# Ten and six weight chunks for the first token tile, with new transfer costs in the planner

## The chip, the cores and the metric

The kernel runs on one core of one Trainium2 chip. Its time is device microseconds from the first to the last instruction of the program, and the median of three runs of the kernel before is 1571.47 us (1571.19 to 1572.18). The engines are TensorE (PE, with PEld for its weight loads), VectorE (DVE), ScalarE (ACT), GpSimd (POOL) and SyncE (SP), which here only issues transfers.

## The reference

An attention with pooled keys and values feeds two feed-forward layers, each `x @ w_in`, an activation, `@ w_out`:

```
k_p, v_p = mean of k, v over groups of 8 positions        # 576 -> 72 keys
attn = softmax(q @ k_p.T / 8) @ v_p                       # 8 batches, 8 heads, 576 x 64
x = attn as 4608 tokens x 512
x = leaky(x @ w_in1, 0.01) @ w_out1                       # 512 -> 2048 -> 512
x = h * clip(h + 3, 0, 6) / 6 @ w_out2, with h = x @ w_in2
```

The weights arrive as 64-bit words and are decoded to float32 on the chip. The kernel makes every large product of three matmuls on split operands (high x high, high x low, low x high).

## The kernel before

The 4608 tokens are nine tiles of 512. Tiles 0 to 2 go through the first layer with ordinary matmuls, one chunk of 128 hidden units after the other (`gemm1` makes a chunk's hidden values, `activate` and `split_g` turn them into `gh` and `gl`, and two steps later `gemm2` adds the chunk's share to four output banks `y0` to `y3`). Tiles 3 to 8, and later the whole second layer, go in pairs through a seven-product scheme (`Pair`, line L1056).

The first layer has 16 weight chunks. Tile 0 is taken in two visits, since its weights are still arriving: the first visit uses the chunks below `C["mid"]`, tile 1 then uses all 16, and a second visit of tile 0 uses the others. The first visit's partial result is stored in between (`yp`). A chunk below `mid` is made by `weights`: a 1 MB load (L655), two ACT instructions (L666, L668) and two DVE instructions (L671, L679) that decode it, a split into high and low half (a cast at L312 or L313 and a subtraction at L322), and a store of the decoded chunk to DRAM (L696, `chunk`), because the pair scheme reads it again later (`first_weights`). A chunk from `mid` on is made in pairs by `pair_weights`, which forms the pair scheme's combinations at once. `keep` (L713) stores each finished chunk's halves to DRAM for the pair scheme.

Raw loads of the chunks 3, 5 and 7 share one buffer (`w14`), as do 4 and 6 (`w15`): `room` says so. The load of chunk 5 can be issued only when ACT has decoded chunk 3, and so on. SP issues all transfers in one queue in the program's order, and a transfer that waits for its buffer holds back those behind it.

A planner (`Plan.order`) makes the order. Every task has an engine and a cost in ns, transfers have a size-dependent cost and a latency until others may use them, and a list scheduler with forward and backward passes puts the tasks in order. Each engine runs its own list strictly in that order. Small copies may go to ACT or to DVE for the first `C["flex"]` tasks. Until the first `gemm2` the planner fills every gap that it foresees on TensorE with dummy matmuls of zeros (`plan.fill`, L1615), one for each 56 ns:

```
if engine == "pe" and busy is not None:
    out += [self.fill] * int((self.starts[i] - busy - 200) / 56)
```

The place where side work is handed to the planner is given by slot numbers in `C` (attention units, weights, preparations).

Of the kernel before, what the change touches and what calls it, by code (L numbers as in the profile page):

```python
# [29 lines left out]
ROUNDS = 12  # L30
C = dict(
    n32=1,
    soon={0: 2000, 1: 4000, 2: 6000},
    flex=536,
    mid=8,
    half0=3,
    steps0='rffrfffr',
    when0=[0, 0, 0, 4, 3, 5, 13],
    att0=[0, 9, 27, 30],
    sec0=4,  # L40
    half1=0,
    steps1='ffffffffffffffff',
    when1=[9, 14, 15, 19],
    att1=[32, 41],
    sec1=23,
    att2=[7],
    quick=[0, 1, 0, 2, 5],
    slow=[0, 4, 5, 5, 4],
    left1=[[(0, 41), (1, 10)], [(2, 4), (3, 3)]],
    att3=[0, 5, 8, 10, 20, 36],  # L50
    gaps3=[0, 2, 2, 2, 0],
    prep3=[17, 48],
    att5=[11, 19, 33, 44, 54, 62],
    gaps5=[0, 3, 2, 9, 4],
    prep5=[94, 156],
    att7=[0, 19, 35],
    gaps7=[1, 12, 11, 13, 18],
    prep7=[87, 97],
    left2=[[(0, 10)], [(1, 16)], [(2, 22)], [(3, 55), (4, 22), (5, 50)], [(6, 18), (7, 51)]],
)  # L60
SCORES = 1700
EXPS = 1782
TRANSPOSES = 260
FIRST_LOADS = 1.25
WARM_FROM = 2700
ENGINES = ("pe", "act", "dve", "gp", "dma")
FIRST = {"dma": 1700.0, "gp": 600.0, "dve": 700.0}


def _f32(bits):  # L70
# [3 lines left out]
class Buf:  # L74


    def __init__(self, plan, pool, tag, shape, dtype, bufs):
        row = plan.tags.setdefault(tag, [])
        self.prev = row[-bufs] if len(row) >= bufs else None
        if self.prev is not None:  # L80
            self.prev.gone = True
        self.gone = False
        row.append(self)
        self.args = (pool, tag, shape, dtype, bufs)
        self.name = f"{tag}_{len(row)}"
        self.tile = None
        self.users, self.writers, self.readers = set(), {}, {}
# [24 lines left out]
class Plan:  # L112
# [8 lines left out]
        ("dve", "dve"): 125,  # L121
        ("act", "act"): 0,
        ("pe", "pe"): 0,
        ("dma", "dma"): 2150,
    }

    def __init__(self):
        self.tags, self.tasks, self.fill_until, self.sooner = {}, [], None, {}
        self.extra, self.landing = [], 0

    def add(self, engine, cost, emit, reads=(), writes=(), other=None):

        n = len(self.tasks)
        after = set()
        over = lambda d, key: (t for k, v in d.items() if all(a == b for a, b in zip(k, key)) for t in v)
        for v in (*reads, *writes):
            assert not v.buf.gone, v.buf.name
            if v.buf.prev is not None:
                after |= v.buf.prev.users
        for v in reads:  # L140
            before = {t for key in v.keys for t in over(v.buf.writers, key)}
            assert before, v.buf.name
            after |= before
        for v in writes:
            for key in v.keys:
                after.update(over(v.buf.writers, key))
                after.update(over(v.buf.readers, key))
        after.discard(n)
        for v in reads:
            for key in v.keys:  # L150
                v.buf.readers.setdefault(key, set()).add(n)
            v.buf.users.add(n)
        for v in writes:
            for key in v.keys:
                v.buf.writers.setdefault(key, set()).add(n)
            v.buf.users.add(n)
        self.tasks.append(([(engine, cost, emit)] + ([other] if other else []), after))
        self.extra.append(self.landing if engine == "dma" else 0)

    def lag(self, a, b):  # L160

        return self.LAG.get((a, b), 1500 if a == "dma" else 1250 if b == "dma" else 180)

    def place(self, ways, after, then, rank, lag, first, back=False):


# [16 lines left out]
        while done < n:  # L183
            best = None
            for e in ENGINES:
                while waiting[e] and waiting[e][0][0] <= free[e]:
                    _, i, k = heapq.heappop(waiting[e])
                    heapq.heappush(ready[e], (rank[i], i, k))
                while ready[e] and way[ready[e][0][1]] is not None:
                    heapq.heappop(ready[e])  # L190
                while waiting[e] and way[waiting[e][0][1]] is not None:
                    heapq.heappop(waiting[e])
                start = free[e] if ready[e] else waiting[e][0][0] if waiting[e] else None
                if start is not None and (best is None or start < best[0]):
                    best = (start, e)
            start, e = best
            free[e] = start
            if not ready[e]:
                continue
            _, i, k = heapq.heappop(ready[e])  # L200
            starts[i], way[i] = start, k
            free[e] = stop = start + ways[i][k][1]
            end = max(end, stop)
            done += 1
            for j in then[i]:
                left[j] -= 1
                late = self.extra[j if back else i]
                for m, w in enumerate(ways[j]):
                    since[j][m] = max(since[j][m], stop + lag(e, w[0]) + late)
                if not left[j]:  # L210
                    offer(j)
        return starts, way, end

    def order(self):
# [19 lines left out]
        for _ in range(ROUNDS):  # L234
            starts, way, end = self.place(ways, after, then, rank, self.lag, FIRST)
            chosen = [w[k] for w, k in zip(ways, way)]
# [20 lines left out]
def attention_moe_moe(ctx: ExitStack, tc: tile.TileContext, qt, kt, vm, vr, wt, wq, eye, mask, out):  # L257
# [15 lines left out]
    plan = Plan()  # L273
    add = plan.add
# [26 lines left out]
        add("pe", n, emit, reads, writes)  # L301

    def on_dma(nbytes, emit, reads, writes):
        add("dma", nbytes / 340 + 60, emit, reads, writes)

    def other(*way):
        return way if len(plan.tasks) < C["flex"] else None
# [19 lines left out]
    def load(dst, src, nbytes):  # L327

        on_dma(nbytes * (FIRST_LOADS if len(plan.tasks) < 60 else 1), lambda: DMA.dma_start(out=dst.ap(), in_=src), [], [dst])

# [317 lines left out]
    left1 = []  # L648
# [4 lines left out]
    def load_w(f, raw):  # L653
        on_dma(
            1 << 20, lambda: DMA.dma_start(out=raw.get().bitcast(I32), in_=wt[ORDER[f]].bitcast(I32)), [], [raw()]  # L655
        )
# [29 lines left out]
    def decode_w(f, raw, t, l):  # L686

        decode(raw, t, l)
        wf = buf(f"w{f}", [128, 4, 512], F32R)
        w[f] = wf  # L690
        hi = wf("hi", lambda t: t[:, 0:2].rearrange("p a n -> p (a n)"))
        lo = wf("lo", lambda t: t[:, 2:4].rearrange("p a n -> p (a n)"))
        copy(hi, t, 1024)
        subtract(lo, t, hi, 1024)
        d = chunk[f]()
        on_dma(1 << 19, lambda: DMA.dma_start(out=d.ap(), in_=t.ap()), [t], [d])  # L696
        keep(f, wf)
# [222 lines left out]
    left2 = Left(2)  # L920
# [489 lines left out]
    for u in units[:3]:  # L1410
        g = u.n % 2
        a = a13 if g else a12
# [11 lines left out]
    load(mask_sb, mask, 1536)  # L1424
    fetch(u1)
    add("dve", 70, lambda: DVE.memset(three.ap(), 3.0), [], [three])
    room = {0: 8, 1: 9, 2: 10, 3: 14, 4: 15, 5: 14, 6: 15, 7: 14}
    temps = {}

    def weights(f):  # L1430
# [42 lines left out]
    mid = C["mid"]  # L1473
# [109 lines left out]
    pairs = [Pair(2 * sum(widths[:i]), n) for i, n in enumerate(widths)]  # L1583
# [20 lines left out]
        for k in range(2):  # L1604
            p.jobs.at(56 + 8 * (3 + 2 * k), lambda nxt=nxt, k=k: nxt.prepare(k))
    for p in [*pairs1, *pairs]:
        plan.landing = 250 if p in pairs else 1300
        if p in pairs:
            p.new_spare()
        p.first()  # L1610
        p.second(p is pairs[-1])
# [66 lines left out]
```

## Time and profile before

| | |
|---|---|
| median of three runs | 1571.47 us |
| the profiled execution | 1572.92 us, span 1571.1 us |
| PE busy | 1564.6 us (100%) |
| DVE, ACT busy | 1157.2 us (74%), 969.7 us (62%) |
| transfers | 406.32 MB, mean 259 GB/s |

PE counts as busy while a matmul is in its pipeline, the dummy matmuls included. So a busy PE is not the same as useful work, and the share of DVE and ACT is an average over stages: both are far busier in the first 110 us than later.

### The profile page before, as it was taken

To read this page: it belongs to the slowest core of one execution; us is meant where nothing else is said; L and a number is where in the kernel's file an instruction comes from. 1 tells how busy PE (TensorE), PEld (TensorE's weight loads), DVE (VectorE), ACT (ScalarE), POOL (GpSimd) and SP (SyncE) were. 2 spreads that over 40 slices of the span, in tenths; PEclk is the share of its full clock that TensorE was granted. 3 is DMA by queue.
4 is the path that set the end of the run, shared out by engine and by line. 5 is a ranking of instruction groups with operands and counts; after the bars stand their busy time and mean duration, and the time that the engine had idled before them with its cause. 6 is when DMAs were issued, how large, how long until landed. Compare 5 with 4: busy or idle time off the path is not lost.

```text
span 1571.1 us, 22819 instructions
## 1 busy us (share of the span) xinstructions
PE 1564.6 (100%) x7971; PEld 1342.9 (85%) x7971; DVE 1157.2 (74%) x2000; ACT 969.7 (62%) x2219; POOL 1.9 (0%) x11
## 2 busy tenths in 40 slices
PE   9999999999999999999999999999999999999999
PEld 8888888888888888888888888898899888889988
DVE  7998568568789776985696579559756856875494
ACT  7886476667877677666655455446545544654454
POOL 0000000000000000000000000000000000000000
PEclk9999999999999999999999999999999999999999
DMA  8899778668896898979976567756866675676564
GB/s 313 298 338 313 256 246 272 211 240 285 286 309 225 294 340 298 325 266 335 320 271 224 200 228 248 254 210 218 291 213 230 236 254 210 228 245 229 210 231 143
DMA packets 128322, 406.32 MB, mean 259 GB/s; under 512 B 18512, under 2 KB 47312, under 8 KB 106448
## 3 DMA queue, kind: packets, MB, share of 16 engines
q1 hardware_dynamic: 128208, 404.87, 74.5%
q8 instruction: 63, 1.03, 0.3%
q14 instruction: 51, 0.42, 0.1%
HBM read 317.79 MB, written 87.03 MB: 258 GB/s over the span
## 4 chain that ended last, share of the span: by engine, by line
PE 95%; DVE 3%; ACT 1%; DMA 1%; issue 0%; SPq 0%; DVEq 0%
PE y L1056 37%; PE h L1056 21%; PE a L1056 12%; PE h L752 3%; PE y L801 3%; PE y L802 3%; PE y L803 3%; PE h L754 3%; PE h L753 3%; PE a L626 2%; PE a L492 2%; DVE w L923 1%; PE a L574 1%; PE idle L1615 1%; PE a L594 1%; DVE gl L1251 0%
## 5 line engine op out<-in xcount | busy, mean ns | idle before, releaser
L923 DVE TENSOR_TENSOR w<-y,w 128x512 f32<-128x512 f32 (+2 forms) x108 | 71.0, 658 | 117.5 <-PE y L1056 115.8
L315 ACT ACTIVATE gh<-w 128x460 fp32r<-128x460 f32 (+1 forms) x140 | 82.2, 589 | 65.2 <-PE y L1056 24.8
L923 DVE TENSOR_TENSOR w<-w 128x460 f32<-128x460 f32 (+2 forms) x168 | 104.9, 645 | 3.4 <-ACT w L767 3.0
L1251 DVE SCALAR_TENSOR_TENSOR gl<-w,gh 128x460 fp32r<-128x460 f32 (+1 forms) x140 | 88.4, 633 | 23.5 <-ACT gh L315 23.2
L1056 PE MATMUL y<-w,xh 128*128 128x512 f32 (+2 forms) x444 | 103.9, 383 | 0.0
L1056 PEld LDWEIGHTS y<-w,xh 128*128 128x128 f32 x444 | 82.6, 188 | 13.0
L312 ACT CAST gh<-w 128x512 fp32r<-128x512 f32 x96 | 59.6, 623 | 41.4 <-PE y L1056 21.5
L1222 ACT ACTIVATE gh<-w,three 128x460 f32<-128x460 f32 (+1 forms) x60 | 40.9, 682 | 71.0 <-DVE w L923 71.0
L1056 PE MATMUL y<-w,raw 128*128 128x460 f32 (+1 forms) x384 | 83.4, 370 | 0.0
L801 PE MATMUL y<-gh,w 128*128 128x512 f32 (+2 forms) x204 | 80.3, 394 | 0.1
L752 PE MATMUL h<-xh,w 128*128 128x512 f32 (+2 forms) x204 | 79.8, 391 | 0.0
L1056 PEld LDWEIGHTS y<-w,raw 128*128 128x128 f32 x384 | 72.1, 188 | 8.2
L802 PE MATMUL y<-gl,w 128*128 128x512 f32 (+2 forms) x204 | 78.3, 384 | 0.0
L803 PE MATMUL y<-gh,w 128*128 128x512 f32 (+2 forms) x204 | 78.2, 383 | 0.0
L753 PE MATMUL h<-xl,w 128*128 128x512 f32 (+2 forms) x204 | 77.9, 382 | 0.0
L754 PE MATMUL h<-xh,w 128*128 128x512 f32 (+2 forms) x204 | 77.9, 382 | 0.0
L1056 PE MATMUL y<-w,xl 128*128 128x512 f32 (+2 forms) x324 | 76.8, 385 | 0.0
L322 DVE TENSOR_TENSOR gl<-w,gh 128x512 fp32r<-128x512 f32 x96 | 65.6, 684 | 12.4 <-ACT gh L312 12.4
L322 DVE TENSOR_TENSOR st<-raw,st 128x512 fp32r<-128x512 f32 x88 | 59.7, 685 | 14.7 <-ACT st L312 14.6
L1056 PE MATMUL y<-gh,raw 128*128 128x462 f32 (+1 forms) x224 | 70.0, 373 | 0.0
L517 ACT ACTIVATE s<-a,mx 128x72 f32<-128x72 f32 x204 | 62.5, 345 | 11.7 <-DVE mx L508 11.7
L1056 PEld LDWEIGHTS y<-w,xl 128*128 128x128 f32 x324 | 60.4, 188 | 10.4
(267 smaller groups left out, 4145.0 us busy)
## 6 DMA issues: line engine op xcount, KB each, us to landing
raw<-left SPq DMA_DIRECT2D x68, 1024.0 KB, 4.8
left<-st SPq DMA_DIRECT2D x176, 256.0 KB, 4.7
xh<-left SPq DMA_DIRECT2D x37, 1024.0 KB, 4.8
xl<-left SPq DMA_DIRECT2D x68, 512.0 KB, 5.1
xh<-left SPq DMA_DIRECT2D x56, 512.0 KB, 5.3
w<-left SPq DMA_DIRECT2D x56, 512.0 KB, 5.2
xl<-left SPq DMA_DIRECT2D x25, 1024.0 KB, 4.9
w<-wt SPq DMA_DIRECT2D x16, 1024.0 KB, 8.2
```

What stands on the lines that cost most here:

```text
L315: a = lambda: ACT.mul(out=dst.ap(), in_=src.ap(), mul=scale)
L322: lambda: DVE.tensor_tensor(out=dst.ap(), in0=a.ap(), in1=f32(b.ap()), op=ALU.subtract),
L517: ACT.activation(out=at()[:, c, h, :], in_=s4()[:, c, pi, :], func=AF.Exp, bias=mx.get()[:, c, h : h + 1], accum_out=sm.get()[:, 4 * c + h ...
L752: PE.matmul(out=o, lhsT=hi, rhs=xh.get()[:, k, c0:c1], start=k == 0, stop=False)
L753: PE.matmul(out=o, lhsT=hi, rhs=xl.get()[:, k, c0:c1], start=False, stop=False)
L754: PE.matmul(out=o, lhsT=lo, rhs=xh.get()[:, k, c0:c1], start=False, stop=k == 3)
L801: PE.matmul(out=y[:, n0:n1], lhsT=hi, rhs=gh.get()[:, n0:n1], start=start, stop=False)
L802: PE.matmul(out=y[:, c0:c1], lhsT=hi, rhs=gl.get()[:, c0:c1], start=False, stop=False)
L803: PE.matmul(out=y[:, c0:c1], lhsT=lo, rhs=gh.get()[:, c0:c1], start=False, stop=stop)
L923: on_dve(n, lambda: DVE.tensor_tensor(out=dst.ap(), in0=a.ap(), in1=b.ap(), op=op), [a, b], [dst])
L1056: PE.matmul(out=o, lhsT=l, rhs=r, start=first and i == m == 0, stop=last and i == len(left) - 1 and m == 2, skip_group_check=True,)
L1251: lambda: DVE.scalar_tensor_tensor(out=lo.ap(), in0=v.ap(), scalar=1.0 / 6.0, in1=f32(hi.ap()), op0=ALU.mult, op1=ALU.subtract),
```

## The change

`mid` becomes 10, so the first visit of tile 0 uses ten chunks and the second six. `steps0` gets two more full steps, `room` two more raw buffers (chunk 8 in `w15`, chunk 9 in `w14`). Three pairs of chunks instead of four are made by `pair_weights`, five instead of four by `first_weights`. The planner's cost of a transfer changes: before, bytes / 340 + 60 ns everywhere, 1500 ns until another engine may read it, and a further `landing` of 250 ns or 1300 ns in the pair stages; now bytes / 420 + 40 ns up to the pair stages, 340 in the first layer's pairs, 400 in the second's, with 2100 ns and `landing` 0, 900 and 0. The first loads lose their factor of 1.25, and the first transfer is assumed to start at 800 ns in place of 1700. Slots, `flex` and the priorities `soon` are new numbers.

```
-    soon={0: 2000, 1: 4000, 2: 6000},
-    flex=536,
-    mid=8,
+    soon={0: 2000, 1: 4000, 2: 10000},
+    flex=436,
+    mid=10,
...
-    steps0='rffrfffr',
+    steps0='rffrfffrff',
...
-FIRST_LOADS = 1.25
+FIRST_LOADS = 1.0
...
-FIRST = {"dma": 1700.0, "gp": 600.0, "dve": 700.0}
+FIRST = {"dma": 800.0, "gp": 600.0, "dve": 700.0}
...
-        ("dma", "dma"): 2150,
+        ("dma", "dma"): 2500,
...
-        return self.LAG.get((a, b), 1500 if a == "dma" else 1250 if b == "dma" else 180)
+        return self.LAG.get((a, b), 2100 if a == "dma" else 1250 if b == "dma" else 180)
...
-        add("dma", nbytes / 340 + 60, emit, reads, writes)
+        add("dma", nbytes / plan.rate + 40, emit, reads, writes)
...
-    room = {0: 8, 1: 9, 2: 10, 3: 14, 4: 15, 5: 14, 6: 15, 7: 14}
+    room = {0: 8, 1: 9, 2: 10, 3: 14, 4: 15, 5: 14, 6: 15, 7: 14, 8: 15, 9: 14}
...
-        plan.landing = 250 if p in pairs else 1300
+        plan.landing, plan.rate = (0, 400) if p in pairs else (900, 340)
```

TensorE's program loses 44 dummy matmuls (203 before, 159 now) and keeps every other matmul; from the middle of the first pair on its order is the same. Before, 73 stand ahead of the first unit's scores, 35 ahead of the second's, 46 from there to the third's, 35 ahead of the first `gemm1`, none between the first two `gemm1` and 14 ahead of the first `gemm2`; now it is 45, 10, 68, 5, 17 and 14.

SP's queue at the start, before (`w8`, `w9` and `w10` receive the raw chunks 0, 1 and 2, `w14` the second unit's values, `w7` its queries and the third's):

```order
L329 DMA raw_2_204<-vm 128x1024
L655 DMA w8_1_264<-wt 128x2048
L329 DMA mask_1_309<-mask 96x4
L329 DMA w14_1_312<-vr 96x512
L655 DMA w9_1_325<-wt 128x2048
L329 DMA w14_1_312<-vm 128x1024
L655 DMA w10_1_395<-wt 128x2048
L329 DMA w7_1_186<-qt 128x768
```

And now:

```order
L329 DMA mask_1_165<-mask 96x4
L329 DMA raw_2_162<-vm 128x1024
L655 DMA w8_1_174<-wt 128x2048
L655 DMA w10_1_226<-wt 128x2048
L655 DMA w9_1_254<-wt 128x2048
L329 DMA w14_1_311<-vr 96x512
L329 DMA w14_1_311<-vm 128x1024
L329 DMA w7_1_98<-qt 128x768
```

Chunk 2 goes ahead of chunk 1, and the second unit's values go behind all three chunks.

The same queue around the load of chunk 5, the third into `w14`, before:

```order
L329 DMA raw_4_597<-vm 128x1024
L655 DMA w15_2_603<-wt 128x2048
L696 DMA chunk2_1_659<-w12_1_70 128x1024
L329 DMA raw_4_597<-vr 96x512
L329 DMA raw_5_687<-kt 128x1152
L655 DMA w14_3_713<-wt 128x2048
```

And now (`left1` is where `keep` stores finished chunks, `w10_2` receives chunk 10):

```order
L655 DMA w10_2_513<-wt 128x2048
L713 DMA left1_10_1_558<-w0_1_381 128x2x256 x2
L696 DMA chunk2_1_567<-w12_1_70 128x1024
L713 DMA left1_200_1_598<-w0_1_381 128x2x256
L713 DMA left1_10_1_558<-w1_1_471 128x2x256
L713 DMA left1_210_1_620<-w1_1_471 128x2x256
L713 DMA left1_250_1_642<-w1_1_471 128x2x256
L655 DMA w14_3_647<-wt 128x2048
```

The load of chunk 10 and six stores of `keep` now stand ahead of the load of chunk 5.

ACT's list at the instruction that reads chunk 5 first, before (`sb_2` are the exponentials of the fifth attention unit, `w11` is what the decode writes):

```order
L517 ACTIVATE sb_2_771,sm_4_772<-a_21_731,mx_4_768 128x72 x6
L767 ACTIVATE u_4_811<-h_6_755 128x128
L312 CAST gh_4_813<-u_4_811 128x128
L668 ACTIVATE w11_1_412<-w14_3_713 128x1024
L767 ACTIVATE u_5_835<-h_7_780 128x512
```

And now:

```order
L312 CAST xh_1_383<-x32_1_342 128x128
L668 ACTIVATE w11_1_356<-w14_3_647 128x1024
L312 CAST w4_1_725<-w12_1_70 128x1024
L517 ACTIVATE sb_2_746,sm_4_747<-a_20_708,mx_4_743 128x72 x6
L517 ACTIVATE sb_2_746,sm_4_747<-a_21_710,mx_4_743 128x72 x6
L312 CAST vbd00_1_81<-raw_4_500 64x2x64
L767 ACTIVATE u_4_791<-h_6_730 128x128
```

The first reader of chunk 5 moves ahead of the unit's exponentials and of the cast of chunk 4.

## Rows read from the trace of the kernel before

**Rows 1.** The page's head: span, then busy time by engine.
```profile
span 1571.1 us, 22819 instructions
...
PE 1564.6 (100%) x7971; PEld 1342.9 (85%) x7971; DVE 1157.2 (74%) x2000; ACT 969.7 (62%) x2219; POOL 1.9 (0%) x11
```

**Rows 2.** Busy time by stretch: us, busy by engine, granted clock, DMA share, GB/s.
```profile
0.00:38.00 38.00, 36.03 (x402) 32.98 (x403) 28.92 (x58) 27.40 (x100) 1.91 (x11) 1.00 0.87 311
38.00:110.00 72.00, 72.00 (x470) 63.02 (x470) 70.89 (x127) 59.16 (x169) 0.00 (x0) 1.00 0.88 317
110.00:200.00 90.00, 90.00 (x414) 73.36 (x413) 65.36 (x108) 55.17 (x126) 0.00 (x0) 1.00 0.86 293
...
1380.00:1400.00 20.00, 19.42 (x91) 16.59 (x90) 15.88 (x30) 12.52 (x24) 0.00 (x0) 1.00 0.81 280
```

**Rows 3.** PE's waits: waited for, us in total, times, longest.
```profile
PE a L492 <- ACT keys L315: 0.5, 1, 0.5
...
PE a L1056 <- ACT gh L315: 0.2, 1, 0.2
```

**Rows 4.** PE in order of time up to the first gemm2: start, us, what.
```profile
0.99 6.91 PE L1615 MATMUL idle<-zeros 128*128 128x128 bf16 x73 [0.99 <-DVE three L1426]
7.83 1.56 PE L492 MATMUL a<-keys,q 64*128 64x72 f32 x24
9.32 2.13 PE L1615 MATMUL idle<-zeros 128*128 128x128 bf16 x35
11.38 1.56 PE L492 MATMUL y<-keys,w 64*128 64x72 f32 x24
...
37.83 0.47 PE L801 MATMUL y<-gh,w 128*128 128x512 f32 x1
```

**Rows 5.** Transfers issued at 1.65, 2.59, 8.41, 10.15, 40.15: KB, us to landing.
```profile
q<-qt SPq DMA_DIRECT2D x1, 384.0 KB, 5.2
w<-kt SPq DMA_DIRECT2D x1, 288.0 KB, 5.8
w<-wt SPq DMA_DIRECT2D x1, 1024.0 KB, 11.0
w<-wt SPq DMA_DIRECT2D x1, 1024.0 KB, 13.0
w<-wt SPq DMA_DIRECT2D x1, 1024.0 KB, 6.2
```

**Rows 6.** ACT in order of time: chunk 1, exponentials, chunk 3, chunk 5.
```profile
22.94 1.17 ACT L666 ACTIVATE w<-w 128x1024 f32<-128x1024 f32 x1
...
31.66 0.31 ACT L517 ACTIVATE s<-a,mx 128x72 f32<-128x72 f32 x1
...
38.22 1.14 ACT L666 ACTIVATE w<-w 128x1024 f32<-128x1024 f32 x1
...
53.73 1.14 ACT L668 ACTIVATE w<-w 128x1024 int32<-128x1024 uint32 x1
```

**Rows 7.** DVE in order of time at the start.
```profile
7.70 0.75 DVE L389 TENSOR_REDUCE w<-w 128x72 f32<-128x576 f32 x1 [2.17 <-DMA w<-kt]
9.42 0.61 DVE L508 TENSOR_REDUCE mx<-a 128x6 f32<-128x432 f32 x1 [0.97 <-PE a L492]
...
30.95 1.11 DVE L508 TENSOR_REDUCE mx<-a 128x6 f32<-128x432 f32 x2
31.98 0.54 DVE L322 TENSOR_TENSOR xl<-x,xh 128x384 fp32r<-128x384 f32 x1
...
37.33 0.49 DVE L322 TENSOR_TENSOR gl<-u,gh 128x384 fp32r<-128x384 f32 x1
```

**Rows 8.** The longest waits of ACT and of DVE, 24 to 110 us.
```profile
ACT st L312 <- DVE raw L923: 4.1, 3, 1.9
...
DVE spill L316 <- ACT x L315: 0.5, 1, 0.5
```

**Rows 9.** Transfers issued from 110 to 120 us: stores of finished chunks.
```profile
DMA packets 3485, 3.41 MB, mean 341 GB/s; under 512 B 718, under 2 KB 3314, under 8 KB 3484
```

More of the change, by code (lines that the diff above doesn't have):

```diff
@@ L32 @@
     n32=1,
-    soon={0: 2000, 1: 4000, 2: 6000},
-    flex=536,
-    mid=8,
+    soon={0: 2000, 1: 4000, 2: 10000},
+    flex=436,
+    mid=10,
     half0=3,
-    steps0='rffrfffr',
-    when0=[0, 0, 0, 4, 3, 5, 13],
-    att0=[0, 9, 27, 30],
+    steps0='rffrfffrff',
+    when0=[1, 1, 1, 2, 10, 6, 13, 15, 19],
+    att0=[0, 9, 20, 34],
     sec0=4,
@@ L42 @@
     steps1='ffffffffffffffff',
[L43 to L52, printed above, removed]
-    att5=[11, 19, 33, 44, 54, 62],
[L54 to L59, printed above, removed]
+    when1=[0, 22, 21],
+    att1=[44, 58],
+    sec1=36,
+    att2=[1],
+    quick=[0, 2, 1, 2, 9],
+    slow=[0, 0, 3, 4, 4],
+    left1=[[(0, 1), (1, 19)], [(2, 5), (3, 4), (4, 14)]],
+    att3=[1, 3, 7, 8, 16, 48],
+    gaps3=[1, 1, 1, 1, 1],
+    prep3=[27, 73],
+    att5=[11, 19, 33, 44, 54, 62],
+    gaps5=[0, 4, 3, 9, 1],
+    prep5=[100, 163],
+    att7=[0, 18, 35],
+    gaps7=[4, 11, 12, 12, 6],
+    prep7=[78, 80],
+    left2=[[(0, 16)], [(1, 22)], [(2, 16)], [(3, 57), (4, 20), (5, 48)], [(6, 13), (7, 60)]],
 )
@@ L128, in __init__ @@
         self.tags, self.tasks, self.fill_until, self.sooner = {}, [], None, {}
-        self.extra, self.landing = [], 0
+        self.extra, self.landing, self.rate = [], 0, 420
     def add(self, engine, cost, emit, reads=(), writes=(), other=None):
```

## The prediction

> **What bounds the kernel now.** I read the page's head first, then the busy time by stretch, then PE's waits, and only then the start in order of time, because the first three say where a gain can be at all. The head says that PE is busy for 1564.6 of 1571.1 us [rows 1]. That could still hide dummies and half-speed stretches, so the reader should look at the stretches: from 38 to 200 us PE is busy for 162 of 162 us at a granted clock of 1.00, and the only stretch after the start with a visible loss is 1380 to 1400, with 0.58 us [rows 2]. PE's waits agree: the longest after the start is 0.5 us, for keys, and the next are of 0.2 us, in that last stretch [rows 3]. The change leaves every matmul but the dummies in place, and in that last stretch it leaves PE's order alone too. So after the start there is at most the 0.5 us to win, and everything else that can move there can only be lost.
>
> The start is different. Up to the first gemm2 at 37.83 us PE is paced by others, and part of its busy time is dummies: 73 of them fill 0.99 to 7.83 us, 35 more 9.32 to 11.38 [rows 4]. There are 203 in all. A dummy has 128 columns, which is 107 ns at 1.2 GHz and 53 at 2.4; the first 73 average (7.83 - 0.99) / 73 = 94 ns and the next 35 average 59 ns [rows 4], so about 53 of the first ran at the lower clock, until about 6.6 us, and the rest at the higher.
>
> DVE is the second thing to know. From 38 to 110 us it is busy for 70.89 of 72 us [rows 2], so it has only 1.1 us in which a delay could vanish. And in that whole time neither ACT nor DVE waited for a transfer: their longest waits are for each other, 4.1 and 0.5 us [rows 8].
>
> **The change, part by part.** The sum is made against the profiled execution, 1572.92 us with a span of 1571.1; the median of the runs is 1571.47, so 1.45 us come off at the end.
>
> *Ten chunks in place of eight in the first visit.* Two chunks are decoded whole instead of in a pair; DVE has 18 instructions fewer, ACT 6 more, SP has two stores of 512 KB and four loads of 256 KB more, 2.1 MB, which is 6.2 us of the queue at 341 GB/s [rows 9]. PE's matmuls are the same. ACT has 12.8 us free from 38 to 110 and queues are busy for 0.88 of it [rows 2]; that covers the work, not its lateness, which comes below. Cost 0.
>
> *Fewer dummies.* 44 go, at 56 ns each 2.5 us. That is what the start would gain if dummies alone held it back. They don't. The first scores need the queries of the first unit, issued at 1.65 us and landed 5.2 us later, at 6.85 [rows 5]; the dummies ended at 7.83. Now 45 dummies end at 0.99 + 45 x 0.107 = 5.8, so the scores start at about 6.9, 0.9 us sooner. But the next step on the path is on DVE: it reduces these scores from 9.42 on [rows 7], and in the new order both reductions of the second unit's keys stand ahead of it. The keys' second half lands at 2.59 + 5.8 = 8.4 [rows 5] and its reduction takes 0.75 [rows 7], so the scores' reduction starts at 9.2. Of 0.9 us, 0.2 are left.
>
> *Chunk 1 behind chunk 2.* Counting the bytes in the queue, chunk 1 was complete after 5.05 MB and landed at 8.41 + 11.0 = 19.4 us, chunk 2 after 6.62 MB at 10.15 + 13.0 = 23.2 [rows 5]. Now chunk 1 is complete after 5.90 MB: by the line between the two, 21.4 us. ACT began its decode at 22.94, with other work ahead of it [rows 6]. Now ACT gets there at about 20 and waits until 21.4. From that instruction to the third unit's exponentials ACT's new list holds 15 more instructions; at their durations in the trace they come to 9.3 us, which ends at 30.7. The exponentials began at 31.66 [rows 6], after the reduction of 30.95 [rows 7], and the third scores come out at nearly the same time as before, so they start about 0.4 us sooner. Behind that reduction DVE loses one xl instruction of 0.5 us (at 31.98) from the path to gl, since all four now stand ahead [rows 7]. Together the gl that starts at 37.33 [rows 7] comes 0.4 to 0.9 us sooner, and with it the first gemm2. I take 0.7 us gained. The ends: 2.5 gained, if the dummies were the brake after all, and 1.0 lost, if chunk 1 lands only when the third load landed before (23.2).
>
> *Transfers costed faster.* This is where the change can lose. The load of chunk 5 was issued at 40.15 and landed 6.2 us later, 46.4 [rows 5]; its first reader on ACT started at 53.73 [rows 6], so 7.3 us were to spare. In the new order this reader stands ahead of 12 exponentials (0.3 us each, 3.6 in all) and of four more instructions, some 5 us sooner, at about 48.5. And the load now stands behind the load of chunk 10, six stores of 256 KB and one of 512 KB, 3.1 MB, at 341 GB/s [rows 9] 9.2 us if all of it is still queued, nothing if it is gone. So it lands between 46.4 and 55.6. Most of it can be issued from 32 us on, while the issue of chunk 5's load still waits for ACT's decode of chunk 3, which ended at 39.4 [rows 6], so I expect 2 us of it to be left: landing at 48.4, just in time. The same holds for chunk 7, whose load waits for the decode of chunk 5, and for chunk 9 behind it. ACT runs its list in order: behind the waiting reader stand the cast of chunk 4 and the unit's exponentials, DVE waits for these, and PE for DVE. Of each such wait DVE's 1.1 us of free time absorb the first. I take 0.6 us lost on PE in this stretch; the ends are 0 and 6 us (three waits of 3 us less what DVE absorbs).
>
> The Trainium skill's page "TensorE: Matmul & The Clock Gate", in the section on the array's architecture, states that ACT and DVE are strict FIFO. In the trace no later ACT instruction passes a waiting one, so rule and trace agree, and the rule speaks against this change: it would make the loss the full wait.
>
> *The rest.* The keys' wait of 0.5 us [rows 3] may go or be another; the pair stages keep their order on PE, and their transfer costs change by less than 0.3 us for 1 MB. I take 0, with ends of -0.5 and +1.0.
>
> **Sum.** 1572.92 - 0.7 + 0.6 + 0 = 1572.8 for a profiled execution, less 1.45: 1571.4; I say 1571.3.
>
> **Rivals.**
>
> *The loads come late.* ACT waits for chunk 5, then for 7, then for 9, and each wait delays the decode that lets the next load go. For it: the three loads share one buffer, DVE has 1.1 us of slack, and a lone 1 MB load took 6.2 us. Against it: 7.3 us to spare before. It decides from a landing of chunk 5 after about 50 us. Price 3 to 8 us, say +5: 1576.
>
> *The start shrinks by all its dummies.* Then 2.5 us and perhaps the keys' 0.5 go: 1568.5. For it: the second scores waited behind 35 dummies to 11.38. Against it: the path by ACT and DVE above.
>
> *The clock.* With 45 dummies PE ends them at 5.8 us, before the clock had risen in the trace (6.6), and then stands idle for 1.1 us. If the clock has not risen, the first scores take 3.0 us in place of 1.5 [rows 4], and gl comes up to 1.5 us later: 1572.9, since ACT's wait for chunk 1 absorbs part. The Trainium skill's page "TensorE: Matmul & The Clock Gate", Part 1, says that the low clock is the default and sustained activity releases it; the trace agrees (lower clock until about 6.6 us, higher after), and the rule speaks for this rival, but no run so far shows the shorter warm-up.
>
> **How the numbers follow.** The forecast (within 1.5 us of before) has a chance of 0.55, late loads 0.22, all dummies 0.15, the clock 0.08. A measurement of this kernel can tell about 0.2%, 3.1 us, from no change. Faster by more than that needs the second rival and a little besides: 0.13. Slower needs most of the first: 0.20. Within: 0.67. The range reaches from most of the second rival, 1568.8, to the middle of the first, 1576.
>
> **What would show it.** Right: the first gemm2 at 37.0 to 37.5 us; scores at 6.9; ACT's decode of chunk 1 at 21 to 22; ACT's reader of chunk 5 waiting for its load by less than 2 us; PE busy for 100% from 110 us on. Wrong: a first gemm2 before 36 us (the dummies were the brake), or PE waits of over 2 us between 50 and 110 us with ACT waiting for raw chunks, or new waits after 110 us.

## The result, and the profile after

The changed kernel takes 1591.33 us, the median of five runs (1589.55 to 1595.49), against 1571.46 us for the kernel before in the same session (1570.22 to 1572.18). The ratio is 1.013, with a 95% interval from 1.0115 to 1.0144. I had forecast 1571.3, with a range to 1576.0: the kernel is 19.9 us slower, and the forecast was wrong.

The page's head, which answers to [rows 1]: span, then busy time by engine.

```profile
span 1589.6 us, 22747 instructions
...
PE 1569.6 (99%) x7927; PEld 1345.6 (85%) x7927; DVE 1153.8 (73%) x1982; ACT 975.9 (61%) x2225; POOL 1.9 (0%) x11
```

PE is busy for 5 us longer, with 44 dummies fewer; the other 13.5 us of the longer span are gaps. The same stretches as in [rows 2], and three short ones at a low clock: us, busy by engine, granted clock, DMA share, GB/s.

```profile
0.00:38.00 38.00, 33.12 (x314) 30.07 (x314) 23.27 (x48) 23.08 (x79) 1.91 (x11) 0.87 0.84 299
38.00:110.00 72.00, 69.17 (x456) 59.79 (x454) 64.97 (x106) 59.48 (x177) 0.00 (x0) 1.00 1.03 367
110.00:200.00 90.00, 87.78 (x420) 71.92 (x421) 57.43 (x95) 53.19 (x128) 0.00 (x0) 0.98 0.59 200
...
8.00:16.00 8.00, 8.00 (x62) 7.54 (x61) 3.01 (x6) 6.19 (x38) 0.00 (x0) 0.50 1.04 371
...
114.00:116.00 2.00, 2.00 (x7) 1.61 (x7) 1.97 (x4) 1.74 (x7) 0.00 (x0) 0.50 1.09 384
...
298.00:300.00 2.00, 2.00 (x6) 1.38 (x6) 1.58 (x3) 1.15 (x3) 0.00 (x0) 0.50 0.71 262
```

Read three things here. From 8 to 16 us PE is busy all the time, at half its clock. From 38 to 110 us DVE has fallen from 70.9 to 65.0 us while the DMA engines have gone from 0.88 to 1.03 of their share: DVE, which had 1.1 us free there before, now has 7, and what has become full is the queue. And all 16 DMA engines together moved 367 GB/s when they were full.

PE's waits, which answer to [rows 3]: what it waited for, us in all, times, longest.

```profile
PE a L626 <- ACT tr L312: 5.2, 2, 3.6
PE a L574 <- DVE s L548: 4.6, 3, 2.1
PE a L492 <- DMA q<-qt: 1.6, 1, 1.6
...
PE y L802 <- DVE gl L322: 0.9, 1, 0.9
```

To see where the time went, I added up all matmuls but the dummies in both traces (7768 recorded in each), every shape at its median spacing in the kernel before, and compared the times at which the same sum is reached. The result is how far PE is behind the kernel before, in us, at times of that kernel; the experiments below are in the same table.

| | 45 | 100 | 118 | 250 | 300 | 360 | 900 | end |
|---|---|---|---|---|---|---|---|---|
| after | 5.3 | 6.3 | 12.3 | 13.6 | 18.1 | 20.2 | 18.6 | 18.3 |
| e1_old_costs | 3.0 | 2.2 | 3.3 | 3.8 | 4.6 | 9.9 | 8.4 | 7.0 |
| e2_new_costs | 8.1 | 8.3 | 11.6 | 11.7 | 14.1 | 14.7 | 14.2 | 13.6 |
| e3_dummies | 2.2 | 3.8 | 8.4 | 9.6 | 12.2 | 13.9 | 12.3 | 11.7 |
| e4_dve_order | 3.8 | 5.9 | 8.5 | 10.1 | 12.5 | 13.9 | 12.3 | 11.8 |
| e5_both | 3.4 | 8.2 | 10.4 | 11.1 | 14.8 | 17.0 | 15.4 | 14.9 |
| e7_tr_ahead | 5.4 | 6.9 | 13.3 | 15.5 | 17.8 | 22.4 | 20.7 | 20.3 |
| e8_first_only | 1.8 | 9.8 | 15.5 | 16.6 | 19.4 | 22.0 | 21.9 | 21.1 |
| e9_rate | -0.3 | -0.4 | 0.1 | 2.4 | 2.5 | 12.3 | 12.9 | 12.9 |
| e12_old_slots3 | 2.4 | 2.2 | 2.8 | 3.5 | 7.6 | 7.7 | 6.4 | 4.9 |
| e14_before_420 | 1.0 | 2.6 | 2.6 | 4.8 | 11.5 | 14.9 | 21.3 | 22.7 |
| e11_lags_old | 4.9 | 11.0 | 17.4 | 25.0 | 29.7 | 37.9 | 39.0 | 41.4 |

So after loses 5.3 us at the start, 6.0 between 100 and 118 us, 4.5 between 250 and 300, 2.1 from there to 360, about 1 us each in the two stretches between these places, and nothing behind them: the pair stages lose nothing. Each row is one profiled execution. Four of them lie over 4 us from the median of their kernel's runs (e4_dve_order 4.3 us below; e8_first_only, e9_rate and e14_before_420 4.3 to 5.8 above), so the rows tell where time goes, and the medians tell how much. I take the places in turn.

*The start.* PE in order of time, which answers to [rows 4], and DVE, which answers to [rows 7]: start, us, what, and in brackets the idle time before it and what ended it.

```profile
0.99 4.12 PE L1615 MATMUL idle<-zeros 128*128 128x128 bf16 x45 [0.99 <-DVE three L1426]
6.70 2.20 PE L492 MATMUL a<-keys,q 64*128 64x72 f32 x24 [1.60 <-DMA q<-qt]
8.83 1.25 PE L1615 MATMUL idle<-zeros 128*128 128x128 bf16 x10
10.01 2.84 PE L492 MATMUL y<-keys,w 64*128 64x72 f32 x24
12.78 5.71 PE L413 MATMUL h<-raw,ident 96*96 96x64 f32 x32
...
21.82 0.85 PE L574 MATMUL a<-ident,s 128*128 128x128 f32 x6 [2.09 <-DVE s L548]
...
43.05 0.47 PE L801 MATMUL y<-gh,w 128*128 128x512 f32 x1
```

```profile
18.53 0.42 DVE L457 TENSOR_TENSOR raw<-h,mask 96x256 f32<-96x256 f32 x1 [4.53 <-PE h L413]
...
20.71 0.96 DVE L548 TENSOR_TENSOR s<-s,inv 128x768 f32<-128x768 f32 x1
```

The scores began at 6.70, as forecast. But PE stood idle before them, and in the middle of these scores the granted clock fell to its lower level (1.2 GHz) and stayed there until past 16 us, though PE had work without a gap. The 32 transposes took 5.7 us; in the kernel before they took 3.4. DVE's list now has L457, which needs these transposes, ahead of the first unit's normalisation (L528 to L548), and DVE stood there for 4.5 us. In the kernel before it stood behind:

```profile
12.87 3.41 PE L413 MATMUL h<-raw,ident 96*96 96x64 f32 x32
...
14.98 0.96 DVE L548 TENSOR_TENSOR s<-s,inv 128x768 f32<-128x768 f32 x1
...
17.96 0.41 DVE L457 TENSOR_TENSOR raw<-h,mask 96x256 f32<-96x256 f32 x1
```

The first gemm2 came at 43.05 us, 5.2 us later than before.

*100 to 118 us.* ACT in order of time:

```profile
103.95 0.49 ACT L312 CAST th<-a 128x384 fp32r<-128x384 f32 x1
109.00 0.66 ACT L668 ACTIVATE st<-w 128x512 int32<-128x512 uint32 x1 [4.57 <-DMA w<-wt]
109.57 1.20 ACT L666 ACTIVATE raw<-w 128x512 f32<-128x512 f32 x2
110.67 0.65 ACT L668 ACTIVATE st<-w 128x512 int32<-128x512 uint32 x1
111.23 0.58 ACT L767 ACTIVATE u<-h 128x512 f32<-128x512 f32 x1
111.71 0.46 ACT L312 CAST tr<-a 96x384 fp32r<-96x384 f32 x1
```

ACT waits for the load of chunk 11, issued at 101.28 us: KB, us to landing.

```profile
w<-wt SPq DMA_DIRECT2D x1, 1024.0 KB, 7.7
```

The planner's cost for it is 2^20 / 420 + 40 = 2537 ns and 2100 ns until its reader, 4.6 us in all. Behind the waiting decode stands tr, and PE waits 3.6 us for tr (its wait above); then the clock is low from 114 to 116 us, which I estimate at another microsecond (2 us of busy PE at half its clock).

*250 to 400 us.* The same pattern, DVE first, then ACT with the reload of the first pair's tile, and PE behind it; the clock is low here as well, from 298 to 300 us (its row above).

```profile
282.34 1.35 DVE L389 TENSOR_REDUCE raw<-raw 128x144 f32<-128x1152 f32 x1 [1.76 <-DMA raw<-kt]
...
290.97 2.62 DVE L923 TENSOR_TENSOR raw<-raw 128x512 f32<-128x512 f32 x4 [1.42 <-DMA raw<-chunk]
```

```profile
374.55 1.14 ACT L312 CAST w<-raw 128x512 fp32r<-128x512 f32 x2 [2.67 <-DMA raw<-x]
375.59 0.47 ACT L312 CAST tr<-a 96x384 fp32r<-96x384 f32 x1
...
376.11 0.36 PE L626 MATMUL a<-tr,vrm 96*128 96x192 f32 x1 [1.61 <-ACT tr L312]
```

My theory was then that the new transfer costs let the planner put readers ahead of their data. The rivals were the ten chunks with their slots, and the start alone (dummies, clock, DVE's order) with the rest as its consequence.

### The profile page after: what moved, and what is told of

Same layout as the page of the kernel before. It is cut to its first block, busy times and chain, and to the rows that moved or that the text cites. A ratio compares the mean times of both kernels' runs of the same rounds, so it can differ in the third digit from the quotient of the medians.

```text
span 1589.6 us, 22747 instructions
## 1 busy us (share of the span) xinstructions
PE 1569.6 (99%) x7927; PEld 1345.6 (85%) x7927; DVE 1153.8 (73%) x1982; ACT 975.9 (61%) x2225; POOL 1.9 (0%) x11
## 3 DMA queue, kind: packets, MB, share of 16 engines
q8 instruction: 63, 1.03, 0.3%
## 4 chain that ended last, share of the span: by engine, by line
PE 81%; DVE 5%; DMA 5%; ACT 2%; issue 1%; SPq 0%; DVEq 0%; ACTq 0%
PE y L1056 36%; PE h L1056 23%; PE a L1056 11%; PE a L626 1%; PE y L801 1%; PE y L802 1%; PE y L803 1%; PE h L752 1%; PE a L492 1%; PE h L753 1%; PE h L754 1%; DMA x<-x 1%; DVE w L923 1%; DMA left<-st 1%; DMA raw<-wq 1%; DMA raw<-chunk 1%
## 5 line engine op out<-in xcount | busy, mean ns | idle before, releaser
L1056 PEld LDWEIGHTS y<-w,xh 128*128 128x128 f32 x444 | 82.7, 188 | 12.9
L322 DVE TENSOR_TENSOR gl<-w,gh 128x512 fp32r<-128x512 f32 x96 | 65.8, 686 | 13.9 <-ACT gh L312 13.5
L312 ACT COPY w<-y 128x512 f32<-128x512 f32 (+2 forms) x88 | 50.2, 576 | 31.2 <-PE y L1056 30.9
```

The source lines that it names most:

```text
L312: a = lambda: ACT.copy(out=dst.ap(), in_=src.ap())
L322: lambda: DVE.tensor_tensor(out=dst.ap(), in0=a.ap(), in1=f32(b.ap()), op=ALU.subtract),
L1056: PE.matmul(out=o, lhsT=l, rhs=r, start=first and i == m == 0, stop=last and i == len(left) - 1 and m == 2, skip_group_check=True,)
```

## The experiments

### Costs or chunks

**e1_old_costs**: after, with the old transfer costs.

```
-        add("dma", nbytes / plan.rate + 40, emit, reads, writes)
+        add("dma", nbytes / 340 + 60, emit, reads, writes)
...      (latencies, landings, first transfer and first loads as before)
```

> The kernel after with ten chunks and its new slots, but planned with the transfer costs of the kernel before (340 GB/s and 60 ns, 1500 ns, 2150 ns, landings of 250 and 1300 ns, first transfer at 1700 ns, factor 1.25). Theory 'costs' (the planner is told that transfers are faster, so it puts readers too early and leaves out dummies): the first gemm2 comes at 37 to 39 us in place of 43.1, no wait of ACT for a load is over 1.5 us up to 120 us, and the time is within 4 us of 1571.5. Rival 'ten chunks' (two more chunks by the first path and the slots that go with them overload the stretch up to 400 us whatever the costs): the start heals, but waits of PE of 6 us or more in all stay between 38 and 400 us, and the time stays above 1580.

Measured 1579.3 us (ratio to before 1.0045, 1.003 to 1.006). **e2_new_costs** is the reverse: the kernel before, with eight chunks and its slots, planned with the new costs.

> The kernel before with eight chunks and its own slots, planned with the transfer costs of the kernel after. Theory 'costs': the first gemm2 comes after 40 us, there are new waits behind loads up to 400 us, and the time is 1580 or more. Rival 'ten chunks': the time is within 4 us of 1571.5 and PE has no new wait over 1 us after 40 us.

Measured 1587.24 us (1.0101, 1.0084 to 1.0118), with the first gemm2 at 48.36 us, as theory 'costs' has it. With 1571.5 and 1591.3 the square is complete: the costs make 12 to 16 us of the loss, ten chunks with their slots 4 to 8. Neither theory of e1_old_costs holds as written: up to 120 us PE loses little more than at the start, though ACT still waits 2.0 us for one load, but the first gemm2 comes at 40.43, and 5.3 us go between 300 and 360.

### The start

**e3_dummies**: after, with 30, 14 and 35 dummies more in its first three runs of them.

```
-                out += [self.fill] * int((self.starts[i] - busy - 200) / 56)
+                out += [self.fill] * self.dummies(int((self.starts[i] - busy - 200) / 56))
+MORE = {0: 30, 1: 14, 2: 35}
```

> The kernel after with more dummies at three places of the start: 75 in place of 45 ahead of the first scores, 24 in place of 10 ahead of the second, 57 in place of 22 behind the first unit's transposes; no other instruction changes its place. Theory 'clock' (PE stands idle for 1.8 us behind its 45 dummies, the granted clock falls to 0.50 from 8 to 17 us, and scores and transposes take twice as long): the clock stays at 1.00, the 32 transposes take 3.4 us in place of 5.7 and end at about 15.5, and the first gemm2 comes at 40 us in place of 43.1; the time falls by 3 us. Rival 'late data' (the values' landing and DVE's list set the start, not PE's speed): the transposes are faster, but the first gemm2 stays at 42.5 to 43.5 and the time falls by less than 1 us.

Measured 1585.57 us (1.0083, 1.0067 to 1.0098). PE at the start, and the windows' row from 8 to 16 us:

```profile
7.25 1.56 PE L492 MATMUL a<-keys,q 64*128 64x72 f32 x24 [0.57 <-DMA q<-qt]
8.74 1.51 PE L1615 MATMUL idle<-zeros 128*128 128x128 bf16 x24
10.52 1.56 PE L492 MATMUL y<-keys,w 64*128 64x72 f32 x24 [0.27 <-DMA w<-qt]
12.01 3.41 PE L413 MATMUL h<-raw,ident 96*96 96x64 f32 x32
...
8.00:16.00 8.00, 7.73 (x109) 7.43 (x107) 4.12 (x8) 6.09 (x38) 0.00 (x0) 1.00 1.03 377
```

The clock stays up, the transposes take 3.4 us, and the first gemm2 comes at 39.96. So 3.1 us of the start are the clock's, as the theory said, and dummies alone keep it up; 2.1 us of the start stay lost. The time fell by 5.8 us, more than the theory had, since some of the later waits came out shorter as well.

**e4_dve_order**: after, with DVE's L457 and what hangs on it behind the normalisation.

```
+MOVES = [([55, 54], 36)]     # tasks: mask product and copy; behind the subtraction of rem
```

> The kernel after with DVE's mask product of the values (L457), the two instructions behind it and two copies moved behind the first unit's normalisation (L528 to L548 and L322); no other engine's list changes, and the dummies stay. Theory 'list' (DVE stands for 4.5 us behind an instruction that waits for PE's slow transposes, with the normalisation ready behind it): DVE normalises from 14 us on, the first transposes of probabilities (L574) start at 18.4 to 19.6 in place of 21.8, the first gemm2 comes 2 to 3 us sooner and the time falls as much, though the clock is still low from 8 to 17 us. Rival 'clock alone': DVE's wait moves to another instruction and the first gemm2 gains less than 1 us.

Measured 1589.14 us (1.0107, 1.0089 to 1.0124). DVE normalised from 14.06 us on, L574 started at 20.05, and the first gemm2 at 41.38: 1.7 us gained, between the two theories. The 2.2 us between the medians are not clear of noise, since the intervals of this kernel and of after overlap. **e5_both** has both edits.

> The kernel after with both edits of the start together: the dummies of e3_dummies and DVE's order of e4_dve_order. The dummies alone brought the first gemm2 from 43.1 to 40.0 us, the order alone to 41.4. Theory 'two causes that add': the first gemm2 comes at 38.0 to 38.8 us, near the 37.8 of before, and the time is 2 us below that with the dummies alone. Rival 'one path' (both only make DVE's one wait of 4.5 us shorter, so the second finds little left): the first gemm2 comes at 39.5 to 40.0 us.

Its first gemm2 comes at 39.32, so the order adds 0.6 us to the dummies, much nearer to one path than to two causes. Its time is 1587.79 us (1.0101, 1.0086 to 1.0116), 3.5 below after and 2.2 above the dummies alone (whose interval overlaps with this one). On the way the waits change places: it is 8.2 us behind at 100 us (after: 6.3), but 10.4 at 118 (12.3). In these three kernels the lists behind the start are those of after, and what the start gives, 1.7 to 3.7 us, seems to reach the end in some form (2.2 to 5.8 us; clear of noise with the dummies, not with the order alone). The larger part of the loss stays.

**e8_first_only** heals the start in another way: the planner assumes the first transfer at 1700 ns again, and the first loads have their factor.

```
-FIRST_LOADS = 1.0
+FIRST_LOADS = 1.25
-FIRST = {"dma": 800.0, "gp": 600.0, "dve": 700.0}
+FIRST = {"dma": 1700.0, "gp": 600.0, "dve": 700.0}
```

> The kernel after with only the assumed start of the transfers back: the first transfer at 1700 ns in place of 800 and the factor of 1.25 on the first loads; the 420 GB/s, the latencies, ten chunks and the slots stay. 70 dummies then stand ahead of the first scores. Theory 'two places' (the assumed start sets the dummies and DVE's list of the first 20 us, the rate sets what happens to loads later): the first gemm2 comes at 38 to 40 us, but 6 us or more are lost between 60 and 400 us, and the time is 1580 to 1588. Rival 'start alone' (later waits only follow from the late start): the later losses shrink with it and the time falls below 1578.

The first gemm2 comes at 38.59, but the time is 1589.75 us (1.0111, 1.0095 to 1.0126), 1.8 above the range of theory 'two places'. 8.0 us are lost between 45 and 100 us and 5.7 up to 118. Here the lists behind the start are other ones too, so this is no clean measure of the start; but with e3_dummies to e5_both it ends the rival of the start alone: 14 to 18 us are lost with the start healed but for 0.8 to 2.1 us.

**e6_before_fewer**: the kernel before, with 45 and 10 dummies in place of 73 and 35.

> The kernel before with the first two runs of dummies cut to the numbers of the kernel after: 45 in place of 73 ahead of the first scores, 10 in place of 35 ahead of the second; nothing else changes. Theory 'clock': PE idles from about 5 to 6.8 us, the granted clock falls to 0.50 by about 8 us and stays there for 8 us or more, the 32 transposes take 5.7 us in place of 3.4, and the first gemm2 comes 2 us or more later than 37.8; the time rises by 2 to 4 us. Rival 'dummies are the brake': the first gemm2 comes 1 to 2.5 us sooner and the time falls as much.

Measured 1574.45 us over ten runs (1.0015, 1.0006 to 1.0024). In the profiled run the first scores waited 2.1 us, the clock was 0.50 from 8 to 20 us, and the first gemm2 came at 41.93, 4.1 us late. Eight runs took 1574.2 to 1575.6, two 1571.1 and 1569.8. The mean granted clock of these two was 0.999 and 1.000, that of seven of the eight 0.996 or 0.997, so the clock seems to have held in the two; the eighth (1575.5) has 1.000 as well, which stays open. **e10_before_62** leaves 62 and 22 of them.

> The kernel before with 62 in place of 73 dummies ahead of the first scores and 22 in place of 35 ahead of the second: enough to reach the queries' landing at 6.8 us, but no more. Theory 'clock holds' (a gap of under 1 us does not let the clock fall): the first scores start at 6.9 to 7.2 us, the clock stays at 1.00, the first gemm2 comes 0.3 to 0.9 us sooner than 37.8, and the time falls by as much, to 1570.6 to 1571.2. Rival 'clock falls' (as with 45 and 10 dummies, where 8 of 10 runs took 1574 to 1576): the time rises to 1573 or more.

Measured 1570.84 us over eleven runs; the ratio of 0.9995 (0.9987 to 1.0004) does not tell it from before. In its profile an idle gap of 0.8 us passed without a fall of the clock, and the first gemm2 came at 36.63, 1.2 us sooner. It is the only version with a median below that of before, and by less than can be told.

### A late load and what stands behind it

**e7_tr_ahead**: after, with the four decodes of chunk 11 behind tr in ACT's list.

```
+MOVES = [([496, 495, 499, 500], 441)]     # tasks: four decodes; behind tr
```

> The kernel after with the four decodes of the weight chunk that is loaded last (L668, two L666, L668, for which ACT waited 4.6 us at 104 us) moved behind the evacuation tr and the activation that stood behind them; SP's and PE's lists stay. Theory 'a late load holds ACT's list, and PE waits for what is queued behind it': PE's wait of 3.8 us at 108.3 us shrinks below 1 us, the clock does not fall after it, and PE is 4 us or more ahead at 120 us, which the end keeps. Rival 'the wait only moves' (gh stands behind the same decode and PE needs it next): a wait of 3 us or more at another instruction before 120 us, and the gain at 120 us is under 1.5 us.

Measured 1591.89 us (1.0127, 1.0112 to 1.0142). PE's wait at tr is gone, and it is 8.9 us behind at 107 us in place of 11.8; but at 118 it is 13.3 behind. PE's waits from 100 to 130 us:

```profile
PE h L752 <- ACT u L767: 1.9, 1, 1.9
PE y L802 <- DVE gl L322: 0.8, 1, 0.8
PE y L801 <- ACT gh L312: 0.5, 1, 0.5
PE h L753 <- DVE xl L322: 0.5, 1, 0.5
```

The rival was right in that what is taken from one wait goes to the next, though in several waits of up to 1.9 us where it had one of 3: the chunk itself comes too late.

**e12_old_slots3**: as e1_old_costs, with the third tile's slots of the kernel before.

```
-    prep3=[27, 73],
+    prep3=[17, 48],
...      (att3, gaps3 and the second weights of this stage as before; fifth chunk pair at slot 6)
```

> Ten chunks planned with the old transfer costs, as in e1_old_costs, but with the slots of the third tile's stage as the kernel before has them (att3, gaps3, prep3, the second weights of that stage), and the fifth chunk pair of the first path at slot 6. In e1_old_costs 5.3 of the 7.0 us are lost between 330 and 360 us, where ACT waits for the reload of the first pair's tile, which is issued at 353 us (337 in the kernel before) and lands 9.4 us later (5.8 before). Theory 'slots' (the slots were chosen for the new costs and put that reload late): it is issued at 345 us or sooner, the loss there falls below 2 us, and the time is 1573 to 1576. Rival 'ten chunks' (the fifth chunk pair of the first path needs that place): the loss stays above 4 us and the time above 1577.

Measured 1577.03 us (1.0037, 1.0026 to 1.0048). The loss from 300 to 360 us is gone (0.1 in place of 5.3), but not as the theory had it: the reload is issued at 351.5, only 1.7 us sooner than in e1_old_costs, and what changed is that it lands in 5.1 us in place of 9.4. And 4.1 us now go between 250 and 300 us, so the time misses the theory's range by 1 us. The slots explain that place, not all that ten chunks cost: some 5 us stay without a cause that I could show.

### The rate

**e9_rate**: after, with one number back.

```
-        self.extra, self.landing, self.rate = [], 0, 420
+        self.extra, self.landing, self.rate = [], 0, 340
```

> The kernel after with one number of the planner back: 340 in place of 420 GB/s up to the pair stages (latencies, start at 800 ns, slots and ten chunks stay). Theory 'rate' (loads and stores that stand one behind the other in the queue are planned too fast, and their readers too early): the loss from 80 to 120 us, 6.6 us in the kernel after, falls below 2 us, and the time comes near the 1579.3 of the kernel planned with all the old costs. Rival 'latency and start' (the first transfer at 800 ns and the latencies do the harm): the time stays above 1586.

Measured 1581.66 us (1.0058, 1.0041 to 1.0074). The same stretches as at the top, and one behind 360 us:

```profile
38.00:110.00 72.00, 71.95 (x467) 62.41 (x467) 68.01 (x114) 61.02 (x167) 0.00 (x0) 1.00 0.92 333
110.00:200.00 90.00, 90.00 (x422) 73.54 (x421) 56.78 (x98) 54.69 (x138) 0.00 (x0) 1.00 0.70 237
...
364.00:374.00 10.00, 8.62 (x41) 6.68 (x41) 7.08 (x12) 7.65 (x17) 0.00 (x0) 0.50 0.71 280
```

PE has next to no gap left from 38 to 200 us, and at 118 us it is 0.1 us behind in place of 12.3. Most of the rest goes at the late reload of e1_old_costs, 9.8 us between 300 and 360. A part of that is the clock's, which fell behind PE's waits there: the profiled execution is the slowest of four (1585.93 us, mean granted clock 0.996), and the two runs with 1.000 took 1579.05 and 1580.94. **e14_before_420** is the other side: the kernel before with 420 in place of 340.

> The kernel before with one number of its planner changed: a transfer costs bytes / 420 + 60 ns in place of bytes / 340 + 60; eight chunks, slots, latencies and the assumed start stay. The other side of e9_rate. Theory 'rate': 60 dummies stand ahead of the first scores in place of 73, readers of loads stand sooner, and PE loses 4 us or more, most of it before 120 us; the time is 1575 or more. Rival 'the rate harms only with ten chunks' (two more loads and stores fill the queue): the time is within 2 us of 1571.5.

Measured 1589.85 us (1.0124, 1.0108 to 1.0139): one number costs 18.1 us, with eight chunks, old slots and old latencies. Only 2.6 us of it go before 120 us, so the theory's place was wrong; most go from 250 us on. It is not quite the change's number: here 420 holds in the pair stages too, where after has 340 and 400, and of the 22.7 us that the profiled execution is behind at its end 7.8 go after 360 us. ACT's waits for transfers from 24 to 400 us, all in the kernel before and the four largest in this one:

```profile
ACT st L312 <- DMA left<-st: 0.6, 1, 0.6
ACT w L312 <- DMA raw<-x: 0.2, 1, 0.2
```

```profile
ACT st L312 <- DMA left<-st: 8.8, 5, 3.2
ACT st L668 <- DMA left<-st: 3.6, 5, 1.9
ACT st L668 <- DMA raw<-wq: 3.5, 1, 3.5
ACT raw L666 <- DMA raw<-wq: 3.3, 1, 3.3
```

**e11_lags_old**: after, with the latencies of 1500 and 2150 ns in place of 2100 and 2500.

> The kernel after with only the latencies back: 1500 ns in place of 2100 from a transfer to its reader on an engine, 2150 in place of 2500 from transfer to transfer; 420 GB/s, the assumed start, ten chunks and slots stay. Theory 'rate': shorter latencies make the plan still more hopeful, and the time stays at 1588 or more. Rival 'latency' (the longer latency harms, since it puts the transfers in another order): the time falls below 1584.

Measured 1612.4 us (1.0263, 1.0243 to 1.0282). In this plan the longer latency of the change was no harm but a remedy: for a lone 1 MB load the old cost is 3.14 + 1.5 = 4.6 us, the new one 2.54 + 2.1 = 4.6 as well. Only where such loads stand one behind the other is the new plan faster. With rate 420 and the short latency it is more hopeful for a lone one too, and it loses twice as much. These two numbers alone don't do it, though: e14_before_420 has both, with eight chunks and the old assumed start, and loses 18.1 us.

Three kernels tell whether 420 is too fast or merely not 340: the kernel before with other rates.

```
-        add("dma", nbytes / 340 + 60, emit, reads, writes)
+        add("dma", nbytes / 300 + 60, emit, reads, writes)     # 300, 345 or 380
```

**r_before_300**

> The kernel before planned with 300 in place of 340 GB/s; nothing else changes. Theory 'hopeful plan' (a planner that is told too fast transfers puts readers ahead of their data; one that is told too slow ones only leaves data waiting): the time is 1572 to 1577, with waits of PE for late data no longer than in the kernel before. Rival 'any other plan' (the slots fit 340 alone, and each other number loses as much as 420, which took 1589.9): the time is 1583 or more.

**r_before_345**

> The kernel before planned with 345 in place of 340 GB/s, a change too small to matter as a cost, but enough for another order on every engine. It shows how much another order alone is worth. Theory 'hopeful plan': within 3 us of 1571.5. Rival 'any other plan': 1578 or more.

**r_before_380**

> The kernel before planned with 380 in place of 340 GB/s, half way to 420. Theory 'hopeful plan': the loss grows with the rate, so it stands between 1571.5 and the 1589.9 of 420, at 1574 to 1584. Rival 'any other plan': as with 300 and 345, with no order among them.

| rate | us | ratio, interval | ACT's waits for transfers, 24 to 400 us |
|---|---|---|---|
| 300 | 1581.6 | 1.0065, 1.005 to 1.008 | 3.1 |
| 340 | 1571.24 | | 0.8 |
| 345 | 1573.89 | 1.0015, 1.0006 to 1.0024 | 6.4 |
| 380 | 1584.26 | 1.0091, 1.0073 to 1.0109 | 12.0 |
| 420 | 1589.85 | 1.0124, 1.0108 to 1.0139 | 23.6 |

Upwards the time and ACT's waits for transfers (the sum of such rows) rise together, as the theory of the hopeful plan has it; DVE's waits for transfers do not (9.5 us at 340, then 17.7, 15.2 and 21.0). Another order by itself costs 2.7 us (345). But 300 loses 10.4 us with few such waits, by the sums of the first table 5.3 of them before 100 us and most of the rest between 500 and 900: that is neither theory's. So the slots of the kernel before fit 340 best of the five, and for the same step the hopeful side loses little more (13.0 us at 380 against 10.4 at 300, with intervals that overlap). How much of 420's loss is hope, and how much is a plan for which the slots were not chosen, these runs do not separate. Of 300's own losses I have no cause.

## Why the prediction was wrong

*The failed step is the third term, transfers costed faster, and how far I let it reach.* I named the mechanism (late loads, ACT's list in order, PE behind it) and took 0.6 us, by one place: the three loads that share a buffer up to 110 us. There I was nearly right: ACT's waits for loads into the two shared buffers (chunks 5, 7 and 8, by the queue's order), from 24 to 110 us, are the last row here, 2.0 us in three, none over 0.8, and PE loses 1.0 us from 45 to 100. Chunk 5 landed at 53.3 us, past the 50 that I had set as the rival's sign, but the start had moved its reader back as well. The first and third row are other transfers.

```profile
ACT st L668 <- DMA w<-wt: 4.6, 1, 4.6
ACT w L312 <- DVE w L679: 2.7, 2, 2.0
ACT w L666 <- DMA chunk<-w: 2.1, 1, 2.1
ACT w L668 <- DMA w<-wt: 2.0, 3, 0.8
```

The load of chunk 11 and the store of a chunk, whose buffer the next decode writes, were not in my sum at all. And all from 118 to 400 us lay in "the rest", at 0, with ends of -0.5 and +1.0. My argument there (pair stages keep their order, their costs change by less than 0.3 us) held for the pair stages, where nothing is lost. But the tiles up to 400 us were planned with 420 too, and 7.9 us went there. In all, the new costs are worth 12 to 16 us, the start included (the square of e1_old_costs and e2_new_costs), and the rate alone 9.7 of them (e9_rate). A number in the planner reaches every stage that is planned with it; I priced it at the place where I had looked.

*The start, -0.7.* It was 5.2 us in the other direction. Scores at 6.9: right (6.70). First gemm2 at 37.0 to 37.5: wrong. Two steps failed. For the clock I asked only whether it had risen when the dummies end (it had, at 4.05 us, sooner than the 6.6 of [rows 4]), and priced half-speed scores alone, 1.5 us. It fell again behind the gap, and 32 transposes ran at half speed too; e3_dummies puts 3.1 us on it. And on DVE I compared what stands ahead of the scores' reduction, but not the list behind it, where L457 had moved ahead of the normalisation. This term makes a quarter of the loss: the three kernels with a better start and the same lists behind it end 2.2 to 5.8 us below after.

*Ten chunks, 0.* With the old costs they lose 7.4 us (e1_old_costs), with the slots of one stage put back 5.2 (e12_old_slots3). I looked at ACT's free time and the queue's share in one stretch, not at the reload of the first pair's tile, which the new slots issue at 353 us or later, amid stores, with 8.2 to 9.4 us to landing (here e1_old_costs):

```profile
raw<-x SPq DMA_DIRECT2D x1, 1024.0 KB, 9.4
```

The kernel before issues it at 337 and has it in 5.8 us.

*The rivals.* "The loads come late" was the right one, at 0.22 and +5 us; its price of 3 to 8 us counted one stretch. The range ended at its middle and left the larger losses out. Of my signs, "new waits after 110 us" came true, and nearly that of PE waits of over 2 us between 50 and 110: the wait of 3.6 us behind chunk 11 begins at 108.6.

## What to carry to other kernels

When a planner's cost changes, compare it with the trace before anything else: the rate that the full queue reached (341 GB/s in [rows 9], 367 after) said that 420 is too fast, and 4.6 us for a 1 MB load, which the old cost gives too, stood beside landings of 6 us and more in [rows 5]. Then price it for every stage that is planned with it, not for the places that the diff makes visible, since each engine's list is in order and a reader put too early holds all that stands behind it. And a wait that is moved aside is not a gain while the data behind it stay late: e7_tr_ahead took away PE's longest one and ended where it was.

The Trainium skill's page "DMA: Bandwidth & Descriptors", in its Specifications, gives a limit of about 358 GB/s for one core's memory, half of what a stack gives two cores, and 435 for the DMA fabric. The rate of 420 lies between them, and this kernel runs on one core, so these two figures do not settle it. The trace does: 367 GB/s over 72 us with full queues, near the lower figure, and 414 over 2 us at the start.

## What was not expected of the hardware

The clock fell again behind shorter gaps than I had reckoned with. At the start it fell to 0.50 after an idle gap of 1.6 us (after) or 2.1 us (e6_before_fewer), and after two shorter ones, of 0.8 and 0.7 us in e7_tr_ahead and of 0.9 us each in e2_new_costs. It held through two gaps of 1.2 and 1.3 us (e9_rate), one of 0.8 (e10_before_62) and one of 0.6 (e3_dummies), and in after through one of 2.1 us ahead of L574. So the length of a gap does not tell alone. Once down at the start, it stayed down for 7 to 14 us (e11_lags_old, e6_before_fewer), about 10 in after, while PE was busy with small matmuls and transposes. And with the same first 45 dummies it rose at 6.6 us in one trace (before) and at 4.05 in another (after). So dummies that end a microsecond before their data did no harm in e10_before_62 and e3_dummies, but the clock fell after two such gaps in e7_tr_ahead and e2_new_costs, and those that end two microseconds before cost 3 to 4 us in most runs of e6_before_fewer.

A transfer of 1 MB took 5.1 us to land when little else was queued (e12_old_slots3) and 7.5 to 9.4 amid stores (after, e1_old_costs); a single figure for its latency is right for neither.
